# Moving three groups of small sums and one norm to other places in the queues of VectorE and GpSimd in an attention and GEGLU kernel

## The chip, the cores and the metric

One Trainium2 chip, one core. The metric is device microseconds (us) of one execution; most executions of one kernel lie within 0.1% of their median. The kernel before takes 303.15 us (median of three runs, 303.06 to 303.15). All runs quoted are of the fast state, with a granted TensorE clock of 0.997 to 1.0.

## The reference, cut to what matters

```python
q_s = softmax(q, axis=-1)               # (8 batches, 8 heads, 576 tokens, 64), float32
k_s = softmax(k, axis=2)
kv  = einsum('bhsd,bhse->bhde', k_s, v)
x   = einsum('bhsd,bhde->bhse', q_s, kv)     # -> (4608 tokens, 512)
h   = gelu(x @ w_gate) * (x @ w_val)         # w_gate, w_val: 512 x 1536
out = h @ w_out                              # 1536 x 512
```

## The kernel before

A *block* is the 512 main tokens of one batch (blocks 0 to 7). The 64 tokens left over in each batch form block 8, which runs ahead of block 7. From block 3 on, the matrix products are done with seven products in place of eight, and these need sums of their operands: sums of x (GpSimd), of the weights (VectorE, once per weight), and of h (VectorE and GpSimd). A step `k.i` is step i of the products for a pair of row groups k and k+3. Letters in the schedule strings are slots for other work; `s0 u0 s1 u1` are sums of h, `10g`, `10v` ordinary gate and value products.

The sums of h; `which` picks the one of four, the first two run on VectorE, the last two on GpSimd:

```python
    def sum_h(j0, j1, which, eng="dve"):
        ...
        for i in which:
            o, a, b, op = {1: (s1, a21, a22, ALU.add), 2: (s2, s1, a11, ALU.subtract),
                           3: (a21, a11, a21, ALU.subtract),
                           4: (s4[:, js], a12, s2, ALU.subtract)}[i]
            (nc.gpsimd if eng == "pool" else nc.vector).tensor_tensor(out=o, in0=a, in1=b, op=op)
    ...
    for b in range(3, B + 1):
        for j in range(NO // 2 - 1):
            at(b, PR, f"s{j}", L(sum_h, j, NO, (1,)), L(sum_h, j, NO, (3,), "pool"))
            at(b, PR, f"u{j}", L(sum_h, j, NO, (2,)), L(sum_h, j, NO, (4,), "pool"))
```

The steps, in short: snapshots (a copy of a bank of partial sums) by ScalarE, adds and finals by VectorE, and the *upper* product (the profile's L649) by GpSimd. In the profile's lines, L605 and L711 are TensorE's products for gate and value and for the output, L575, L586 and L592 the sums of h, of the weights and of x, L643 the adds of the steps (into `eq` or `cc` by turns) and L749 the adds of the output stage (into `yo`). Step k.4 overwrites the bank that step k.3's second add reads, so TensorE waits for that add:

```python
        elif i == 3:
            product_gv(7, pa, xt, k, False)
            add(cc[:, 1], pa, s5)                   # VectorE
            product_gv(2, pb, xt, k, False)
            final(pb, k)                            # ScalarE, VectorE
            ... upper(cc)                           # ScalarE, then GpSimd (L649)
        else:
            product_gv(4, pa, xt, k, False)         # TensorE waits for add(cc[:, 1])
```

The output stage of a block has slots NS 0 to 4 between its products. Product 4 overwrites the bank that the last *yo add* reads:

```python
        s5 = snap("c")
        ride(b, NS, 1)
        product(6, ps["a"], False, js=js)
        s2 = snap("a")
        ride(b, NS, 2)
        product(3, ps["c"], False, js=js)
        add("c", s2, 0, 1)
        ride(b, NS, 3)
        ...
        product(7, ps["a"], False, js=js)
        add("a", s5, 1, 1)                          # the yo add
        ride(b, NS, 4)                              # x of the next block, then its sums
        ...
        product(4, ps["a"], False, js=js)           # waits for the yo add
```

The remainder's norm: a reduce and a reciprocal on VectorE, a multiply (the profile's L273) on GpSimd:

```python
    def norm_rem0():
        nc.vector.reduce_sum(rq, e, axis=mybir.AxisListType.X)
        nc.vector.reciprocal(out=rrq, in_=rq)
        nc.gpsimd.tensor_tensor(out=e, in0=e, in1=..., op=ALU.mult)
```

The softmax here doesn't subtract the row's maximum and nothing guards it: scores larger than these inputs give would overflow.

## Time and profile before

| engine | busy us before | share of the span | instructions |
|---|---|---|---|
| TensorE | 285.7 | 95% | 2401 |
| VectorE | 220.8 | 73% | 418 |
| ScalarE | 188.2 | 63% | 305 |
| GpSimd | 184.3 | 61% | 169 |

Busy shares don't tell what an order of instructions is worth here. I use one measure throughout: a **hole** is the distance between the starts of two matmuls in TensorE's timeline, less the steady distance (0.109 us after a matmul of 256 columns, 0.216 after one of 512). It is some 0.15 us larger than the idle time in the profile's brackets, since matmul ends are modelled. The prediction below shows the lines for the four holes concerned.

### The profile page before, as it was taken

The numbers are of one execution on the slowest core, as the hardware profiler recorded it, in microseconds if no ns is written. First come the engines' busy times: TensorE is split into PE (matmuls) and PEld (weight loads), VectorE is DVE, ScalarE is ACT, GpSimd is POOL, SyncE is SP. The second block draws the span as 40 slices with busy tenths as digits, with TensorE's granted clock in tenths as the row PEclk, the third lists the DMA queues.
The fourth block names the chain that finished last, engine by engine and source line by source line (L and its number), as shares of the span: only waits on it lengthen the run. The fifth ranks groups of instructions, "written<-read, shape, count | busy, mean of one in ns | idle before, by whom it ended". The sixth has DMA issues, their size and how long they took to land. (4 is left out here: it accounts for less than half of the span.)

```text
span 301.0 us, 6201 instructions
## 1 busy us (share of the span) xinstructions
PE 285.7 (95%) x2401; PEld 198.5 (66%) x2401; DVE 220.8 (73%) x418; ACT 188.2 (63%) x305; POOL 184.3 (61%) x169
## 2 busy tenths in 40 slices
PE   3999999999999999899899999998999997999994
PEld 1444445447744586568677867786768886888784
DVE  2953478998677889868967796779678556936792
ACT  3763467767652566567775887587861686438740
POOL 1567557870346009677796779778966596614660
PEclk9999999999999999999999999999999999999999
DMA  7999999996189106950498049903130300033003
GB/s 228 372 383 390 401 388 395 328 309 177 74 301 302 28 35 226 351 89 2 161 377 179 2 140 366 194 2 138 30 70 2 142 1 3 0 70 71 2 1 142
DMA packets 54622, 51.72 MB, mean 172 GB/s; under 512 B 18496, under 2 KB 50496, under 8 KB 54592
## 3 DMA queue, kind: packets, MB, share of 16 engines
q1 hardware_dynamic: 52864, 49.49, 52.1%
q10 hardware_dynamic: 1728, 1.84, 1.9%
q8 instruction: 19, 0.31, 0.4%
q14 instruction: 11, 0.09, 0.1%
HBM read 37.75 MB, written 9.44 MB: 157 GB/s over the span
## 5 line engine op out<-in xcount | busy, mean ns | idle before, releaser
L466 PE MATMUL psg<-xt,wg_sb 128*128 128x512 f16 x216 | 57.4, 379 | 0.0
L466 PE MATMUL psv<-xt,wv_sb 128*128 128x512 f16 x216 | 57.4, 379 | 0.0
L249 POOL TENSOR_TENSOR eq<-eq,rrq 128x640 f16<-128x640 f16 (+1 forms) x27 | 34.9, 1310 | 21.4 <-DVE rrq L242 9.0
L711 PEld LDWEIGHTS <-ht 128*128 128x128 f16 x384 | 37.3, 98 | 9.3 <-issue 4.2
L471 ACT ACTIVATE gl<-psg 128x512 f32<-128x512 f32 x36 | 21.0, 598 | 28.9 <-PE psg L466 28.6
L472 DVE SCALAR_TENSOR_TENSOR ht<-psv,gl 128x512 f16<-128x512 f32 x36 | 24.2, 684 | 16.0 <-PE psv L466 13.7
L466 PEld LDWEIGHTS <-wv_sb 128*128 128x128 f16 x216 | 21.0, 98 | 22.3 <-issue 0.2
L466 PEld LDWEIGHTS <-wg_sb 128*128 128x128 f16 x216 | 21.0, 98 | 20.7
L575 POOL TENSOR_TENSOR s<-ht,sh 128x512 f16<-128x512 f16 x18 | 21.9, 1215 | 10.8 <-DVE sh L575 10.8
L605 PEld LDWEIGHTS <-wv_sb 128*128 128x128 f16 x216 | 20.8, 98 | 11.5 <-issue 4.2
L188 POOL CAST v<-vt 128x640 f16<-128x640 f32 x26 | 20.0, 810 | 12.2 <-PE pskv L342 10.5
L649 POOL TENSOR_TENSOR ht<-eq 128x512 f16<-128x512 f32 x13 | 16.5, 1272 | 17.0 <-ACT eq L647 17.0
L711 PE MATMUL psa<-tw,ht 128*128 128x256 f16 x192 | 23.4, 272 | 2.2 <-DVE yo L749 2.2
L575 POOL TENSOR_TENSOR ht<-ht 128x512 f16<-128x512 f16 x18 | 21.2, 1179 | 6.1 <-DVE sh L575 6.1
L605 PEld LDWEIGHTS <-wg_sb 128*128 128x128 f16 x216 | 21.1, 98 | 2.5
L212 ACT ACTIVATE ek<-kt 128x1280 f16<-128x1280 f32 (+1 forms) x11 | 19.1, 1748 | 5.7 <-DMA kt<-in_k_dram 4.2
L592 POOL TENSOR_TENSOR xs<-xt 128x512 f16<-128x512 f16 x8 | 9.5, 1191 | 21.1 <-ACT xt L190 21.1
L659 ACT COPY pgb<-pga 128x512 f32<-128x512 f32 x27 | 15.9, 590 | 10.4 <-PE pga L605 10.2
L711 PEld LDWEIGHTS <-sh 128*128 128x128 f16 x192 | 18.8, 98 | 2.5 <-issue 0.3
L633 DVE SCALAR_TENSOR_TENSOR ht<-pga,glq 128x256 f16<-128x256 f32 x27 | 11.2, 422 | 12.5 <-ACT glq L632 12.5
L632 ACT ACTIVATE glq<-pgb 128x256 f32<-128x256 f32 x27 | 10.2, 378 | 16.0 <-PE pgb L605 9.5
L212 ACT ACTIVATE eq<-qt 128x2560 f16<-128x2560 f32 (+2 forms) x10 | 18.4, 1863 | 2.7 <-DMA qt<-in_q_dram 2.6
(161 smaller groups left out, 675.1 us busy)
## 6 DMA issues: line engine op xcount, KB each, us to landing
out_dram<-yo SPq DMA_DIRECT2D x15, 512.0 KB, 3.5
kt<-in_k_dram SPq DMA_DIRECT2D x7, 640.0 KB, 8.4
vt<-in_v_dram SPq DMA_DIRECT2D x7, 640.0 KB, 5.2
qt<-in_q_dram SPq DMA_DIRECT2D x7, 640.0 KB, 7.0
qt<-in_q_dram SPq DMA_DIRECT2D x8, 512.0 KB, 7.4
wost<-in_moe_w_out_dram SPq DMA_DIRECT2D x6, 512.0 KB, 7.9
kt<-in_k_dram SPq DMA_DIRECT2D x6, 512.0 KB, 9.7
vt<-in_v_dram SPq DMA_DIRECT2D x6, 512.0 KB, 5.7
```

The lines of the kernel that those rows point to most:

```text
L188: nc.gpsimd.tensor_copy(out=dst, in_=src)
L212: nc.scalar.activation(out=dst[:, n0:NC, h0 * D:h1 * D].rearrange(o, d=D, **({"t": 2} if b >= QUAD else {})), in_=heads(tiles[(nm, b)], b, ...
L249: (nc.gpsimd if eng == "pool" else nc.vector).tensor_tensor(out=e, in0=e, in1=rrq.unsqueeze(-1).to_broadcast((P, n, 2, D)), op=ALU.mult)
L466: nc.tensor.matmul(ps, w[:, ci, fi * P:(fi + 1) * P], xt[:, ci, :], start=(ci == 0), stop=(ci == HP - 1))
L471: nc.scalar.activation(out=gl, in_=psg, func=ACTF.Gelu)
L472: nc.vector.scalar_tensor_tensor(out=ht[:, fi, :], in0=psv, scalar=_H_SCALE, in1=gl, op0=ALU.mult, op1=ALU.mult)
L575: (nc.gpsimd if eng == "pool" else nc.vector).tensor_tensor(out=o, in0=a, in1=b, op=op)
L605: nc.tensor.matmul(ps[:, t], a, x, start=(first and t == 0 and c == 0), stop=(c == 1), skip_group_check=True)
L633: nc.vector.scalar_tensor_tensor(out=ht[:, fi, 0:256], in0=ps[:, 0], scalar=_H_SCALE, in1=gl, op0=ALU.mult, op1=ALU.mult)
L649: (nc.vector if k == NFI - NO // 2 - 1 else nc.gpsimd).tensor_tensor(out=ht[:, k:k + NO // 2 + 1:NO // 2, 256:512], in0=cc[:, :, 0], in1=c ...
L659: nc.scalar.copy(out=pb, in_=pa)
L711: nc.tensor.matmul(ps[t], a, w, start=(first and j == js[0] and (t == ts[0] or ps[t].tensor is not ps[ts[0]].tensor)), stop=(j == js[-1]), ...
```

## The change

Its intent is to take work of VectorE and GpSimd out of the way of what TensorE waits for: the sums of h in block 3 each a step or two later (part 1), the weight sums of blocks 4 to 6 spread over the slots, with two on GpSimd (part 2), the remainder's norm behind block 6's x (part 3), and the sums of x of block 7 behind block 8's sums of h (part 4).

```diff
-    THREE = ("a 6g l 6v 0.1 9g 0.2 9v 0.3 7g 0.4 n 1.1 t 7v s0 u0 1.2 10g 1.3 10v 1.4 s1 u1 2.1 8g"
-             " 2.2 8v 2.3 11g 2.4 11v")
+    THREE = ("a 6g l 6v 0.1 9g 0.2 9v 0.3 7g 0.4 n 1.1 t 7v 1.2 s0 10g 1.3 u0 10v 1.4 2.1 s1 8g"
+             " 2.2 u1 8v 2.3 11g 2.4 11v")
...
-    at(5, NS, 3, norm_rem0)
...
         at(b, NS, 4, L(unit_x4, n, ("act", "dve"), 0 if n == B - 1 else None))
...
+        if b == 5:
+            at(b, NS, 4, norm_rem0)
...
         at(b, NS, 4, L(lambda n: sum_x(get_x(n)), n if n < B - 1 else B))
-    at(6, NS, 4, L(lambda: sum_x(get_x(B - 1), xs_b[1])))
+    at(B, NS, 2, L(lambda: sum_x(get_x(B - 1), xs_b[1])))
...
-    for b, i, what in ((4, 2, "g1 g2"), (4, 3, "g4"), (5, 2, "v1 v2"), (6, 1, "v4"),
-                       (6, 2, "g3 v3")):
-        for x in what.split():
-            at(b, NS, i, L(sum_wgv, x[0], int(x[1]), NO + 1, 2))
+    for b, i, x in ((4, 1, "g1"), (4, 2, "g2"), (5, 1, "v1"), (5, 2, "v2"), (6, 1, "g4"), (6, 2, "v4"),
+                    (6, 2, "g3"), (6, 2, "v3")):
+        at(b, NS, i, L(sum_wgv, x[0], int(x[1]), NO + 1, 2, "pool" if x[1] == "3" else "dve"))
```

Cut: `sum_wgv` takes an argument that picks its engine.

More of the change, by code (lines that the diff above doesn't have):

```diff
@@ L575, in sum_h, with sum_wgv @@
             (nc.gpsimd if eng == "pool" else nc.vector).tensor_tensor(out=o, in0=a, in1=b, op=op)
-    def sum_wgv(nm, i, k=0, n=NO // 2):
+    def sum_wgv(nm, i, k=0, n=NO // 2, eng="dve"):
         w = wg_sb if nm == "g" else wv_sb
@@ L585, in sum_wgv @@
                        3: (a21, a11, a21, ALU.subtract), 4: (t[2], a12, t[1], ALU.subtract)}[i]
-        nc.vector.tensor_tensor(out=o, in0=a, in1=b, op=op)
+        (nc.gpsimd if eng == "pool" else nc.vector).tensor_tensor(out=o, in0=a, in1=b, op=op)
     def sum_x(xt, xs=xs):
```

## The prediction

> **What bounds the kernel now.** I read the busy line of the page first, then TensorE's waits, then its timeline by start times. TensorE is the bound:
>
> ```profile
> PE 285.7 (95%) x2401; PEld 198.5 (66%) x2401; DVE 220.8 (73%) x418; ACT 188.2 (63%) x305; POOL 184.3 (61%) x169
> ```
>
> The change adds and removes no matmul, so it can only fill holes in TensorE's stream. The waits of TensorE name two groups of holes after the start-up:
>
> ```profile
> PE pga L605 <- DVE eq L643: 3.2, 2, 1.8
> PE psa L711 <- DVE yo L749: 2.2, 3, 0.9
> ```
>
> Modelled ends hide part of a hole, so I measured each one by starts. A steady 256-column matmul starts 0.109 us after the last one, a 512-column one 0.216. What exceeds that after 20 us adds up to 11.4 us, much of it row-packed small matmuls that no order changes. The holes concerned are these (TensorE's timeline; the bracket is idle time and releaser):
>
> ```profile
> 128.45 0.38 PE L605 MATMUL pga<-xs,wv_sb 128*128 128x256 f16 x2 [1.81 <-DVE eq L643]
> ...
> 175.24 1.47 PE L711 MATMUL psa<-tw,ht 128*128 128x256 f16 x12 [0.46 <-DVE yo L749]
> ...
> 206.10 1.47 PE L711 MATMUL psa<-tw,ht 128*128 128x256 f16 x12 [0.92 <-DVE yo L749]
> ...
> 250.91 0.38 PE L605 MATMUL pga<-xs,wv_sb 128*128 128x256 f16 x2 [1.35 <-DVE eq L643]
> ```
>
> By starts they are 1.97 us (block 3, step 1.4), 0.62 (end of block 4), 1.08 (end of block 5) and 1.51 (block 8, step 1.4): 5.2 us in all. Each part of the change aims at one. A fifth hole, 0.96 us at 144.83 (end of block 3), is not touched.
>
> **What the Trainium skill says.** "SBUF — State Buffer", section "Who interferes with whom": a VectorE instruction with two SBUF inputs contends with a GpSimd instruction that reads SBUF; the one that starts first holds the shared pair for the whole instruction and the other fully blocks. The trace agrees. The sums of h are such instructions, and normally take 0.42 us; in block 3, on VectorE and then on GpSimd:
>
> ```profile
> 124.63 1.16 DVE L575 TENSOR_TENSOR sh<-ht 128x512 f16<-128x512 f16 x1
> 125.83 1.37 DVE L575 TENSOR_TENSOR sh<-sh,ht 128x512 f16<-128x512 f16 x1
> 127.12 0.68 DVE L643 SCALAR_TENSOR_TENSOR eq<-pgc,snq 128x512 f32<-128x512 f32 x1
> 127.72 0.68 DVE L643 SCALAR_TENSOR_TENSOR eq<-pga,snq 128x512 f32<-128x512 f32 x1
> ...
> 124.25 2.67 POOL L249 TENSOR_TENSOR eq<-eq,rrq 128x640 f16<-128x640 f16 x2 [1.66 <-DVE rrq L242]
> 126.88 1.33 POOL L575 TENSOR_TENSOR ht<-ht 128x512 f16<-128x512 f16 x1
> ```
>
> The first GpSimd norm (1.26 us alone) ends near 125.51, the first sum at 125.79; the second norm ends at 126.9, the second sum at 127.20. Each sum ends 0.28 us after the GpSimd instruction it met. "TensorE: Matmul & The Clock Gate", section "Architectural detail: the array is 16× 32×32, not 1× 128×128", has VectorE, ScalarE and GpSimd as strict FIFO: what is placed earlier holds up what stands behind it. The last two VectorE lines show it: both adds were ready and stood behind the sums. "GPSIMD Engine Reference", section 8, calls VectorE about twice as fast on elementwise work; here a 128x512 sum is 1.15 us on GpSimd and 0.42 on VectorE.
>
> **Part 1, sums of h of block 3.** In the new order VectorE does add 1.2, sum s0, add 1.3, final of 1.3, sum u0, ... Add 1.2 at 124.63 to 125.23; s0 meets the first norm and still ends at 125.79; add 1.3 ends at 126.4. Step 1.4 on TensorE could start at 126.48, so the 1.97 us hole closes. But GpSimd's order changes too: the upper product of 1.3 (L649) now precedes u0's GpSimd sum. By durations from the timeline: s0's GpSimd sum to 128.2, L649 to 129.44, u0's sum to 130.56. Sum s1 on VectorE waits for L649, and by 129.48 u0's sum has the port, so s1 ends at 130.56+0.28=130.85; add 2.2 takes 0.6; u1 meets s1's GpSimd sum (130.9 to 132.06) and ends at 132.34; 8v 0.6; add 2.3 ends at 133.54. Step 2.4, formerly at 134.09, wants 134.09-1.97=132.12 and gets 133.59. Gain **0.5 us**; 1.47 of the 1.97 comes back one pair later.
>
> **Part 2, one weight sum per snapshot, blocks 4 and 5.** Five sums of 0.33 to 0.82 us leave the stretch ahead of the last yo add; one goes into the 0.6 us VectorE idles before the snapshot at 171.58. Block 6, whose add is not held up, has 2.26 us from the first matmul of product 7 to that of product 4 (233.95 to 236.21). Block 4 has 2.55, block 5 3.01. So product 4 comes 0.29 us earlier in block 4, and 0.75 in block 5 if the remainder's norm leaves too. Yet step 1.4 of the next block hangs on another chain: x on ScalarE, four sums of x, four norms and two L649 on GpSimd, s0, add 1.3 on VectorE. In block 5 that ends at 190.30 and step 1.4 starts at 190.46. TensorE 0.29 earlier would want 190.17 and gets 190.35: **0.1 us** stays. Block 6's sums g3 and v3 on GpSimd fit its idle time from 232.45 to 236.96: 2 times 1.15 us. Nothing.
>
> **Part 3, the remainder's norm behind x.** Block 5's product 4 gains its 0.75. Now GpSimd's multiply (1.03 us) waits for a reduce and reciprocal that stand behind VectorE's x copies, and the sums of x stand behind it. GpSimd before, then the sum it releases:
>
> ```profile
> 205.56 1.03 POOL L273 TENSOR_TENSOR eq0r<-eq0r,rrq 64x512 f16<-64x512 f16 x1 [0.92 <-DVE rrq L272]
> 206.55 1.15 POOL L592 TENSOR_TENSOR xs<-xt 128x512 f16<-128x512 f16 x1
> ...
> 211.12 4.93 POOL L249 TENSOR_TENSOR eq<-eq,rrq 128x640 f16<-128x640 f16 x4
> 216.01 1.27 POOL L649 TENSOR_TENSOR ht<-eq 128x512 f16<-128x512 f32 x1
> 217.23 1.27 POOL L649 TENSOR_TENSOR ht<-cc 128x512 f16<-128x512 f32 x1
> ...
> 218.53 0.42 DVE L575 TENSOR_TENSOR sh<-ht 128x512 f16<-128x512 f16 x1 [1.00 <-POOL ht L649]
> ```
>
> GpSimd has no gap from 205.56 to 218.5. After: VectorE's yo 204.60 to 205.20, copies to 206.6, multiply 0.98 later at 207.58, first sum of x at 208.57: 2.02 us late. Step 0.1 wants its first sum at 208.82, gets it at 209.77: 0.95 lost. s0 comes 2.02 late, add 1.3 ends at 221.09+2.02=223.11, and step 1.4 starts at 223.16 where it had 221.32. Net **loss 1.84 us**, block 5's gain included.
>
> **Part 4, sums of x of block 7 behind block 8's sums of h.** Four GpSimd sums, 241.53 to 246.10, stand ahead of the L649 that block 8's s0 waits for. Block 7 runs the same steps without them: its hole at the same step is 0.18 us, not 1.51. In the new place GpSimd is idle from 264.6 on; the first sum would end at 265.8 and is wanted at 267.36. Gain **1.33 us**.
>
> Sum: -0.5 -0.1 +1.84 -1.33 = **-0.1 us**, 303.05.
>
> **Rivals.** (A) The intended result: every hole closes and nothing new opens, -1.97-0.29-0.75-1.33=-4.3, 298.8. For it: the holes are real, and the new order in block 3 resembles that of blocks 4 to 6, which have no hole at 1.4. Against it: GpSimd's unbroken chain in block 6, and slack of 0.1 to 0.2 us at step 1.4. (B) Sum s1 gets the port ahead of u0's GpSimd sum: it ends near 129.9, add 2.3 near 132.6, and block 3 gains 1.5 instead of 0.5: 302.0. For it: the semaphore comes as the port is freed. Against: GpSimd's queued instructions follow with no gap in the trace. (C) The late sums of x delay the step less, because GpSimd makes up time: 301.5. Against: its chain has no gap to make it up in. (D) Part 4 moves its wait into block 7: 304.4. Against: 1.5 us of slack.
>
> **Range and chances.** The risks beside the sum lie mostly on the fast side (B one in three for 1.0 us, C one in seven for 1.6, A small), so I go 0.35 us below it: 302.7, range 301.3 to 303.5. A 2% gain is 6.1 us, more than the four holes hold; a 2% loss would need three parts to turn bad.
>
> **What would show it.** Right if: no wait at 1.4 of block 3, but one of some 1.5 us at its 2.4, with s1 and u1 over 1 us on VectorE; waits of product 4 at the ends of blocks 4 and 5 near 0.2 us; in block 6 a wait for sums of x at 0.1 and one of some 1.6 us at 1.4, with the sums starting some 4 us after x's first matmul instead of 2.06; block 8's hole near 0.2. Wrong if block 6 has no new wait or block 3 keeps its full 1.97.

## The result, and the profile after

The kernel after takes **303.10 us** (median of four runs, 302.84 to 303.13), the kernel before 303.11 in the same rounds: ratio 0.9999, 95% interval 0.9982 to 1.0017. Here and below a ratio compares the fast runs of both kernels in the same rounds, as the timing program gives it; it is not quite the ratio of the medians quoted.

Nothing in the time tells of the change. The profile does. TensorE's waits in the kernel after (us in total, times, longest):

```profile
PE pga L605 <- DVE eq L643: 1.5, 1, 1.5
PE pga L605 <- DVE cc L643: 1.3, 1, 1.3
PE psa L711 <- DVE yo L749: 1.2, 3, 0.8
PE pgc L605 <- POOL xs L592: 0.8, 1, 0.8
```

The two waits for adds are there as before, but they are others: one for `cc`, which is step 2.3 of block 3, and one for `eq` in block 6. A wait for sums of x is new. TensorE's timeline of the kernel after:

```profile
133.82 0.38 PE L605 MATMUL pga<-xs,wv_sb 128*128 128x256 f16 x2 [1.30 <-DVE cc L643]
...
205.18 1.47 PE L711 MATMUL psa<-tw,ht 128*128 128x256 f16 x12 [0.16 <-DVE yo L749]
...
209.61 0.38 PE L605 MATMUL pgc<-xs,wsv 128*128 128x256 f16 x2 [0.80 <-POOL xs L592]
...
223.00 0.38 PE L605 MATMUL pga<-xs,wv_sb 128*128 128x256 f16 x2 [1.48 <-DVE eq L643]
```

Holes by starts, in us:

| where | before | predicted | after |
|---|---|---|---|
| block 3, step 1.4 | 1.97 | 0 | 0 |
| block 3, step 2.4 | 0 | 1.47 | 1.47 |
| end of block 3, products 7 and 4 | 0.96 | 0.96 | 1.17 |
| end of block 4, product 4 | 0.62 | 0.33 | 0.32 |
| block 5, step 1.4 | 0 | 0.18 | 0.20 |
| end of block 5, product 4 | 1.08 | 0.33 | 0.32 |
| block 6, step 0.1 | 0 | 0.95 | 0.96 |
| block 6, step 1.4 | 0 | 1.64 | 1.64 |
| block 8, step 1.4 | 1.51 | 0.18 | 0.18 |
| sum | 6.14 | 6.04 | 6.26 |

(A 0 is a hole below 0.05 us. The predicted 0.33 are the old holes less 0.29 and 0.75.)

**Block 3.** VectorE in the kernel after, around sums s1 and u1 (L575):

```profile
129.70 1.36 DVE L575 TENSOR_TENSOR sh<-ht 128x512 f16<-128x512 f16 x1 [1.34 <-POOL ht L649]
130.98 0.68 DVE L643 SCALAR_TENSOR_TENSOR cc<-pgc,snq 128x512 f32<-128x512 f32 x1
131.58 0.99 DVE L575 TENSOR_TENSOR sh<-sh,ht 128x512 f16<-128x512 f16 x1
```

and GpSimd in the same stretch of the same kernel:

```profile
128.40 1.26 POOL L649 TENSOR_TENSOR ht<-eq 128x512 f16<-128x512 f32 x1
129.63 1.14 POOL L575 TENSOR_TENSOR s<-ht,sh 128x512 f16<-128x512 f16 x1
131.14 1.16 POOL L575 TENSOR_TENSOR ht<-ht 128x512 f16<-128x512 f16 x1 [0.36 <-DVE sh L575]
```

L649 ends at 129.66 and releases s1 on VectorE at 129.70; but GpSimd's next sum, which was ready, is already under way since 129.63. It ends at 130.77 and s1 at 131.06, 0.29 us after it.

**Block 6.** GpSimd in the kernel after, from the remainder's multiply to the second upper product:

```profile
207.41 1.03 POOL L273 TENSOR_TENSOR eq0r<-eq0r,rrq 64x512 f16<-64x512 f16 x1 [2.94 <-DVE rrq L272]
208.41 1.15 POOL L592 TENSOR_TENSOR xs<-xt 128x512 f16<-128x512 f16 x1
...
219.08 1.27 POOL L649 TENSOR_TENSOR ht<-cc 128x512 f16<-128x512 f32 x1
```

The first sum of x starts 4.09 us after x's first matmul (204.32); before it was 2.06. GpSimd idles 2.94 us ahead of the multiply, where it had idled 0.92, and all that follows is late by as much.

**Block 8.** GpSimd's upper product and VectorE's s0 in the kernel before:

```profile
246.10 1.26 POOL L649 TENSOR_TENSOR ht<-eq 128x512 f16<-128x512 f32 x1
248.63 0.43 DVE L575 TENSOR_TENSOR sh<-ht 128x512 f16<-128x512 f16 x1 [2.07 <-POOL ht L649]
```

and the same upper product in the kernel after:

```profile
245.35 1.27 POOL L649 TENSOR_TENSOR ht<-eq 128x512 f16<-128x512 f32 x1 [2.14 <-ACT eq L647]
```

Before, the upper product came straight behind the sums of x, and s0 waited 2.07 us for it and the one after it. After, GpSimd is idle ahead of it, and s0 (248.13) waits for nothing.

### The profile page after: what moved, and what is told of

Its sections match the earlier page's. It is cut to its first block, busy times and chain, and to the rows that moved or that the text cites. A ratio compares the mean times of both kernels' runs of the same rounds, so it can differ in the third digit from the quotient of the medians.

```text
span 301.3 us, 6202 instructions
## 1 busy us (share of the span) xinstructions
PE 287.0 (95%) x2401; PEld 198.8 (66%) x2401; DVE 219.5 (73%) x416; ACT 187.8 (62%) x305; POOL 186.7 (62%) x171
## 3 DMA queue, kind: packets, MB, share of 16 engines
q10 hardware_dynamic: 1728, 1.84, 1.9%
## 5 line engine op out<-in xcount | busy, mean ns | idle before, releaser
L575 POOL TENSOR_TENSOR s<-ht,sh 128x512 f16<-128x512 f16 x18 | 21.8, 1214 | 10.9 <-DVE sh L575 10.9
L649 POOL TENSOR_TENSOR ht<-eq 128x512 f16<-128x512 f32 x13 | 16.6, 1274 | 15.4 <-ACT eq L647 15.4
L575 POOL TENSOR_TENSOR ht<-ht 128x512 f16<-128x512 f16 x18 | 21.0, 1165 | 6.2 <-DVE sh L575 6.2
```

The source lines that it names most:

```text
L649: (nc.vector if k == NFI - NO // 2 - 1 else nc.gpsimd).tensor_tensor(out=ht[:, k:k + NO // 2 + 1:NO // 2, 256:512], in0=cc[:, :, 0], in1=c ...
```

## The experiments

All ten gave correct results and ran on chips that also ran the kernel before.

**norm_back.** The kernel after with part 3 undone:

```diff
+    at(5, NS, 3, norm_rem0)
...
-        if b == 5:
-            at(b, NS, 4, norm_rem0)
```

> The kernel after, with the remainder's norm back at its old place (ahead of the yo add of block 5). Theory (part 3 costs 1.84 us by holding up GpSimd's sums of x): 1.84 us under the kernel after, so 301.3 us; block 5's product 4 has its old hole of 1.08 us, block 6 has no wait for sums of x at step 0.1 and no hole at step 1.4. Rival (the parts are worth nothing one by one, TensorE's 95% is the bound, so removing one changes nothing): 303.1 us.

Measured: 300.61 us against 302.97, ratio 0.9924 (0.9910 to 0.9939). Both waits in block 6 are gone, so part 3 is what costs. It costs more than expected, 2.5 us against the kernel after (2.4 by holes) and not 1.84, since block 5's hole is 0.42 us and not 1.08. VectorE in the kernel before, with v1 (kt<-wv_sb) and v2 (kt<-kt,wv_sb) ahead of the first add:

```profile
202.59 0.61 DVE L586 TENSOR_TENSOR kt<-wv_sb 128x512 f16<-128x512 f16 x1
203.23 0.82 DVE L586 TENSOR_TENSOR kt<-kt,wv_sb 128x512 f16<-128x512 f16 x1
203.98 0.68 DVE L749 SCALAR_TENSOR_TENSOR yo<-psc,sn 128x512 f32<-128x512 f32 x1
...
205.40 0.65 DVE L749 SCALAR_TENSOR_TENSOR yo<-psa,sn 128x512 f32<-128x512 f32 x1
```

VectorE in norm_back:

```profile
203.03 0.68 DVE L749 SCALAR_TENSOR_TENSOR yo<-psc,sn 128x512 f32<-128x512 f32 x1
203.64 0.67 DVE L270 TENSOR_REDUCE rq<-eq0r 64x8 f32<-64x512 f16 x1
204.34 0.20 DVE L272 RECIPROCAL rrq<-rq 64x8 f32<-64x8 f32 x1
204.45 0.65 DVE L749 SCALAR_TENSOR_TENSOR yo<-psa,sn 128x512 f32<-128x512 f32 x1
```

With v1 gone to an earlier slot (part 2) the first add starts 0.07 us after its product's last matmul ends in the profile (202.97), where it had started 0.72 us after it, and reduce and reciprocal fit between the two adds but for 0.1 us.

**norm_behind_sums.** The kernel after with the norm one place later, behind the sums of x:

```diff
-        if b == 5:
-            at(b, NS, 4, norm_rem0)
...
         at(b, NS, 4, L(lambda n: sum_x(get_x(n)), n if n < B - 1 else B))
+        if b == 5:
+            at(b, NS, 4, norm_rem0)
```

> The kernel after, with the remainder's norm one place later still, behind the four sums of x in GpSimd's queue. Theory (the loss is head-of-line blocking in GpSimd's queue: 1.46 us of idling for the reciprocal, which the sums now fill): sums of x start at 206.1 by the clock of the kernel before and not at 208.5; no wait at 0.1; only the 1.0 us multiply remains in the chain to step 1.4 of block 6, whose hole falls from 1.64 to some 1.1 us by starts; 1.46 us under the kernel after, 301.6 us. Rival (what costs is the reduce on VectorE behind the x copies, which pushes the next norms' reduces): nothing changes, 303.1 us.

Measured: 301.73 us, ratio 0.9959 (0.9944 to 0.9974). The reduce on VectorE is where it was in the kernel after; only GpSimd's queue differs. GpSimd in norm_behind_sums:

```profile
205.89 1.15 POOL L592 TENSOR_TENSOR xs<-xt 128x512 f16<-128x512 f16 x1 [1.52 <-ACT xt L190]
...
210.47 1.03 POOL L273 TENSOR_TENSOR eq0r<-eq0r,rrq 64x512 f16<-64x512 f16 x1
211.47 4.92 POOL L249 TENSOR_TENSOR eq<-eq,rrq 128x640 f16<-128x640 f16 x4
```

The wait at 0.1 is gone and the hole at 1.4 falls from 1.64 to 1.20 us. What is left fits the multiply's own 1.0 us in the chain: norm_mid, where the multiply is elsewhere, has 0.19 there. The larger part of the loss (1.4 of 2.5 us) is thus a queue whose head waits.

**norm_mid.** The kernel after with the norm in block 5's slot s1, registered behind that slot's sums of h:

```diff
-        if b == 5:
-            at(b, NS, 4, norm_rem0)
...
+    at(5, PR, "s1", norm_rem0)
```

> The kernel after, with the remainder's norm in the middle of block 5, behind sum s1, where VectorE idles 1.1 us and GpSimd 0.98. Theory: block 5 keeps the 0.75 us at product 4 and block 6 loses nothing but about 0.15 at step 1.4, so 0.6 us under the kernel before in this part and 2.45 under the kernel after: 300.65 us. Rival (block 5's gain is always given back in block 6 since GpSimd's chain ends at 1.4 anyway): 301.3 us, as with the norm at its old place.

Measured: 300.58 us, ratio 0.9920 (0.9903 to 0.9936), holes 0.32 (end of block 5) and 0.19 (1.4 of block 6), as expected, and its rival (301.3) is out. It is the same time as norm_back's, though, which has 0.42 and 0.09 at the two holes: the 0.1 us won at product 4 is given back at 1.4. So the run shows a second place for the norm that avoids part 3's loss, but doesn't tell the two places apart.

**only_norm.** The kernel before with part 3 alone; the diff is part 3's in the change.

> The kernel before with the move of the remainder's norm alone. Theory: 1.84 us slower than before, 304.95 us, with the waits at 0.1 (0.95) and at 1.4 (1.64) of block 6. Rival (parts are worth nothing one by one, or the loss needs the other parts): 303.1 us.

Measured: 304.91 us (304.89 to 304.96) against 302.97, ratio 1.0063 (1.0048 to 1.0078). TensorE's waits in only_norm:

```profile
PE pga L605 <- DVE eq L643: 4.6, 3, 1.8
...
PE pgc L605 <- POOL xs L592: 0.8, 1, 0.8
```

A third wait for an add and the one for sums of x: holes of 0.96 at 0.1 and 1.64 at 1.4 of block 6.

**only_three.** The kernel before with part 1 alone, the new `THREE` string.

> The kernel before with the new order of block 3 alone. Theory (the hole at 1.4 closes and 1.47 us comes back at 2.4, as sum s1 meets u0's GpSimd sum at the shared port): 0.5 us faster less what the next hole takes, 302.6 us. Rival (the whole 1.97 us hole is won): 301.1 us.

Measured: 302.77 us (20 runs, 302.47 to 302.97) against 303.06 (31 runs), ratio 0.9990 (0.9983 to 0.9997). The hole of 1.97 us is gone and one of 1.48 stands at 2.4. The end of block 3 loses 0.2 us more (1.16 for 0.96), which the expectation left open: g1 and v1 meet GpSimd's casts at other moments, and the snapshot ahead of product 7 comes late.

**only_sumx.** The kernel before with part 4 alone.

> The kernel before with the sums of x of block 7 moved alone. Theory: block 8's hole at 1.4 falls from 1.51 to 0.18 us and no wait opens in block 7: 1.33 us faster, 301.8 us. Rival (the wait moves into block 7, whose step 0.1 waits for the sums): 303.1 us.

Measured: 301.72 us, ratio 0.9959 (0.9944 to 0.9974). Of TensorE's waits for the adds of steps one is left, block 3's; block 8's hole is 0.18 us and block 7 has no new one. In only_sumx:

```profile
PE pga L605 <- DVE eq L643: 1.8, 1, 1.8
```

**port_free.** The kernel after with GpSimd's sums of h in block 3 in another order; VectorE's order is untouched:

```diff
+            if b == 3:
+                at(b, PR, f"s{j}", L(sum_h, j, NO, (1,)))
+                at(b, PR, f"u{j}", L(sum_h, j, NO, (2,)))
+                continue
...
+    at(3, PR, "s0", L(sum_h, 0, NO, (3,), "pool"))
+    at(3, PR, "u1", L(sum_h, 1, NO, (4,), "pool"), L(sum_h, 1, NO, (3,), "pool"))
+    at(3, NS, 0, L(sum_h, 0, NO, (4,), "pool"))
```

> The kernel after, with GpSimd's queue in block 3 reordered so that no GpSimd instruction is ready when sums s1 and u1 run on VectorE: u0's GpSimd sum goes to the start of the output stage, s1's behind u1. VectorE's order is unchanged. Theory (shared port): s1 and u1 take some 0.43 us each instead of 1.36 and 0.99; the hole at 2.4 falls from 1.47 to some 0.1 us; 1.4 us under the kernel after, less up to 0.2 by a new collision of the last sums in the output stage: 301.7 to 301.9 us. Rival (VectorE simply has too much work in this stretch, or s1 is late only since it waits for L649): hole at 2.4 stays over 1 us, 303.1 us.

Measured: 302.30 us (12 runs) against 303.06, ratio 0.9977 (0.9968 to 0.9985). VectorE in port_free, s1 and u1, then the first sum of h in the output stage:

```profile
129.77 0.43 DVE L575 TENSOR_TENSOR sh<-ht 128x512 f16<-128x512 f16 x1 [1.35 <-POOL ht L649]
...
130.87 0.42 DVE L575 TENSOR_TENSOR sh<-sh,ht 128x512 f16<-128x512 f16 x1
...
135.12 1.14 DVE L575 TENSOR_TENSOR sh<-ht 128x512 f16<-128x512 f16 x1
```

and the GpSimd sum that this last one meets, in the same kernel:

```profile
134.82 1.16 POOL L575 TENSOR_TENSOR s<-ht,sh 128x512 f16<-128x512 f16 x1
```

s1 waits for L649 as long as in the kernel after (1.35 us), but runs 0.43 us instead of 1.36, and the hole at 2.4 falls from 1.47 to 0.12. So it was the port, not the wait for L649 and not too much work. Only 0.8 of the 1.35 us arrive: the GpSimd sum now collides in the output stage, and the hole at product 4 there grows from 1.00 to 1.52. The expectation had allowed 0.2 for this and it took 0.6 in all.

**best1.** The kernel after with the edits of norm_mid and port_free.

> The kernel after with both cures: the remainder's norm in the middle of block 5 and GpSimd's queue of block 3 reordered. Theory: 2.45 and 1.3 us add up, 299.3 us. Rival (gains are given back at the next tight chain, as in the change): 300.6 us or more.

Measured: 299.85 us, ratio 0.9897 (0.9882 to 0.9912). The gains of norm_mid and port_free add up; that it isn't 299.3 is port_free's 0.6.

**only_wgv.** The kernel before with part 2 alone.

> The kernel before with the weight sums of blocks 4 to 6 moved alone, the remainder's norm at its old place. The run norm_back left a hole of only 0.42 us at the end of block 5 where 1.08 was expected, so the step of the prediction that gave 0.75 us there to the leaving norm is in doubt. Theory now: either move by itself frees VectorE for the yo add of block 5, since the sum v1 that leaves lets the add of c and the reduce start 0.66 us earlier; holes 0.32 (end of block 4), 0.2 (1.4 of block 5), 0.42 (end of block 5); gain 0.1+0.66 less up to 0.2 at 1.4 of block 6: 302.4 us. Rival (the prediction's step: block 5 gains only when the norm leaves): 303.0 us.

Measured: 302.30 us (9 runs) against 302.97, ratio 0.9980 (0.9970 to 0.9990). The holes are 0.32, 0.20 and 0.42 as expected. Part 2 alone wins most of what part 3 was meant to win in block 5 (0.66 of 0.75 us).

**best2.** best1 with four weight sums of block 3 a slot later:

```diff
+    for x in ("g4", "v4"):
+        at(3, NS, 4, L(sum_wgv, x[0], int(x[1]), NO, 1))    # ahead of x of block 4
...
-    for b, i, what in ((3, 1, "g1 v1"), (3, 2, "g2 v2 g3 v3"), (3, 3, "g4 v4")):
+    for b, i, what in ((3, 1, "g1 v1"), (3, 2, "g2 v2"), (3, 3, "g3 v3")):
```

> best1 with block 3's weight sums of the last two snapshots each one place later (g3 and v3 behind the add of c, g4 and v4 behind the yo add and ahead of the x copies). Theory (the 1.52 us hole at the end of block 3 is VectorE's queue of eight weight sums, two of them held up by GpSimd's casts): the hole falls to some 0.7 us, and step 1.4 of block 4 has slack for it; 0.8 us under best1, 299.05 us. Rival (given back at 1.4 of block 4, as in blocks 5 and 6): 299.8 us.

Measured: **298.91 us** (four runs, 298.75 to 299.02) against 302.97, ratio 0.9862 (0.9846 to 0.9879). It beats both kernels by 1.4%. The hole at the end of block 3 is 0.59, and TensorE's waits in best2 name no add of a step any more; of the kinds shown so far only this is left:

```profile
PE psa L711 <- DVE yo L749: 0.8, 3, 0.4
```

## Why the prediction was right, point by point

- **The total.** The sum of the parts said 303.05, the stated time after the allowance for risks 302.7; measured 303.10. The allowance was the worse number. That the sum meets the time within 0.05 us is partly luck: the interval of the ratio is 0.5 us to either side, and by holes the change loses 0.12 us where the sum had a gain of 0.10, since 0.2 us at the end of block 3 was missed.
- **Part 1, 0.5 us.** The hole moved to 2.4 with the size worked out (1.47); s1 took 1.36 us and u1 0.99, just under the "over 1 us" forecast. The 0.2 us lost at the end of block 3 was missed; only_three gives 0.3. That the port is the cause is shown by port_free. Rival B (s1 gets the port first) is out: GpSimd's next instruction had started 0.07 us ahead.
- **Part 3, loss of 1.84 us.** Confirmed alone (only_norm, 1.94 by medians, 1.84 by holes) and by its two waits. That the head of GpSimd's queue is the cause is shown by norm_behind_sums. Rival C, that GpSimd makes up time, is out.
- **Part 4, 1.33 us.** Confirmed alone (1.34 by medians). Rival D is out.
- **Part 2, 0.1 us: a step that failed.** The prediction gave block 5's 0.75 us to part 3 ("0.75 in block 5 if the remainder's norm leaves too"). Part 2 alone leaves a hole of 0.42 of 1.08 and so takes 0.66 of it. I had kept the first add at its old start, 203.98 (the forecast "yo 204.60" stands right behind it), though v1's leaving lets it start 0.66 us earlier. Inside the change the error cancels, as both parts are there. Outside it doesn't: part 2 is worth 0.67 us alone, and undoing part 3 wins 2.5 us, not 1.84.
- **Rival A, every hole closes.** best2, which closes most of them, reaches 298.9 where A had put the change (298.8), but only by keeping the new holes from opening and cutting block 3's.
- The parts alone sum to -0.29-0.67+1.94-1.34=-0.36 us by medians, the whole gives -0.01. The 0.66 us that parts 2 and 3 both win in block 5 counts twice in that sum; what is left (0.3 us) is within the interval of the ratio. By holes it closes: the parts alone give -0.29-0.66+1.84-1.33=-0.44. Add the 0.66 counted twice, and take off the 0.10 that only_wgv has at step 1.4 of block 6, where part 3 has its own hole: +0.12, as in the table.

Open: why the last collisions at the end of block 3 take 0.2 us in the kernel after was read from the timelines only, not tested by itself. There, step 2.4 and the start of g1 (140.13 before, 139.86 after) come 0.27 us earlier, but g1 runs 0.60 us instead of 0.40 beside a GpSimd cast that ends only 0.07 earlier (140.39, 140.31), and the yo add and product 4 (144.83, 144.76) come only 0.07 earlier too.

## What to carry to other kernels

Moving an instruction on one engine moves the head of another engine's queue: look up what stands behind it there, and how much slack the next thing that TensorE waits for has (here 0.1 to 0.2 us). A hole that closes makes TensorE early, and the next chain that was just in time becomes the new hole, so follow the shift until something absorbs it. When a change comes out at zero, undo its parts one at a time: here one part of four cost some 2.4 us and hid what the others had won.

## What the Trainium skill lacked or had wrong

- "SBUF — State Buffer", section "Who interferes with whom": the page lets issue order decide who blocks, and both cases here agree. A VectorE sum that was already waiting got the port between two queued GpSimd instructions (ending 0.28 us after the first, before). What the page doesn't say is who wins when the end of a GpSimd instruction itself releases the VectorE sum and GpSimd has another one queued: in the kernel after GpSimd's next started first (129.63, VectorE 129.70), at this one place.
- "GPSIMD Engine Reference", section "8. Key points": VectorE about twice as fast for elementwise work, with no type or size given there. For a 128x512 sum in 16 bits it was 1.15 us to 0.42, a factor of 2.7.
